# Turning the input chunks in SBUF before stage 1 of a Fourier mixing kernel

## The chip, the cores and the metric

The kernel runs on one core of a Trainium2 chip. A core has a matrix engine (TensorE, PE in the profile, with its weight loads listed as PEld), VectorE (DVE), ScalarE (ACT), GpSimd (POOL) and SyncE (SP), which run in parallel and wait for each other on semaphores. Each engine takes its instructions in order. Data lie in SBUF (128 partitions); matmuls write to PSUM. Transfers between HBM and SBUF are DMAs, issued here by SP (queue q1, "hardware") or by POOL (queue q0, "software", which can change the type of the data on the way), and run by 16 DMA engines that all queues share.

The metric is the time of one execution on the device in microseconds (us); lower is better.

## The reference

Input x is 8 batches of 3200 positions and 256 channels, float32. Two steps follow one another:

```python
X = np.fft.rfft(x, axis=1)
y = np.fft.irfft(X * (filt_r + 1j * filt_i)[None], n=3200, axis=1)     # circular filter, per channel
gate = 1 / (1 + np.exp(-causal_conv5(y, conv_w)))                      # 5 taps, per channel
out = (gate * (y @ w_val)) @ w_out
```

`causal_conv5` stands for the sum over k of `conv_w[k] * yp[:, k:k+S]`, where yp is y with four zero positions ahead. The output is float32, 8 x 3200 x 256.

## The kernel before, in words

**The transform.** 3200 is 128 x 25, and the position is written as n = 25 a + 128 r (mod 3200), a below 128 and r below 25. A transform of length 3200 is then one of length 128 over a and one of length 25 over r, with no factors between them. `load_x` (L80) brings a batch into a buffer `xb` with a as the partition: for each r one or two DMAs of rows, 49 in a batch, issued by POOL, which turn float32 into bf16. A row of `xb` is 25 x 260 elements (R x UW): 256 channels, and four columns of zeros. There are three such buffers.

**The channels** are split as d = 52 j + g, j below 5 and g below 52. One matmul takes one g, with all 25 r and 5 j: 125 columns. Eight chunks of a batch (`CH`) hold six or seven g each, 52 in all. The steps, by function:

- `s1` (L315): for each g of a chunk, the 125 columns are the stationary operand (the weights) and the table of cosines and sines `cf_t` (128 columns) is the moving one. In `xb` the columns of one g lie 52 elements apart. DVE evicts the result to `sob` (L324).
- `s2` (L327): the transform over r, four matmuls with tables of 125 x 125; ACT evicts (L338); DVE multiplies with the filter tables `fr_t` and `fm_t` and adds: `za`, `zb`, `z` (L349, L351, L352).
- `inva` (L356): back over r; ACT evicts to `u` (L370), one u per batch.
- `invb` (L375): back over the 128, per piece of three or four r (seven pieces to a batch); ACT evicts to `y` (L390). The first piece of a batch has POOL copy the four positions that the causal convolution needs ahead (L395, L397). It needs all of u.
- `conv` (L399, gate, ACT L411), `val` (L416, times the gate, DVE L428), `outp` (L434; even pieces are evicted by DVE, L445, odd ones by ACT, L448; SP stores them).

All PSUM tiles come from one pool of four buffers, so a tile's matmuls wait until the tile four places earlier has been evicted.

**The order.** The main loop (L470) counts chunks G over all batches, 64 in all. In a step each function handles another chunk or piece: `s1` chunk G, `s2` chunk G-1, `inva` chunk G-3, `invb`, `conv`, `val` and `outp` with lags of 11, 13, 14 and 15. In the loop they stand as invb, s1, conv, s2, val, inva, outp. A scheduler puts out the final order of each engine; on TensorE it is the order just given. Loads for later batches are put out ahead of each step, eight steps early.

**Before the loop** the tables are computed on DVE and ACT, and the filter is transformed to the layout of `fr_t` and `fm_t`. For each of its parts (real, imaginary) 13 x 65 rows are loaded straight (`gf`) and 12 x 65 more (`gh`) are reversed by matmuls (L233) and evicted into `gf` (L239 on ACT for the real part, L241 on DVE for the imaginary one). 52 matmuls turn `gf` (L249), again with 125 columns that lie 52 elements apart as weights; they are evicted to `ft` (L257, L259), and 25 matmuls (L270) expand that for the 25 residues, evicted by L284, L286 and L287.

Of the kernel before, what the change touches and what calls it, by code (L numbers as in the profile page):

```python
# [16 lines left out]
L = 128  # L17
# [14 lines left out]
def kernel(  # L32
# [36 lines left out]
    NX = 3  # L69
    xb = [cpool.tile([128, R, UW], BF16, name=f"xb{i}") for i in range(NX)]  # L70
    SW = 130
    sob = [cpool.tile([128, 7, SW], BF16, name=f"sob{i}") for i in range(4)]
    xsb = [cpool.tile([128, 2, 7, W], BF16, name=f"xsb{i}") for i in range(3)]
# [6 lines left out]
    def load_x(b, r):  # L80
        xt = xb[b % NX]
        na = min(L, -(-(S - L * r) // R))
        for a0, a1, s in ((0, na, L * r), (na, L, L * r + R * na - S)):
            if a1 > a0:
                src = bass.AP(tensor=x.tensor, offset=x.offset + (b * S + s) * D,
                              ap=[[R * D, a1 - a0], [1, D]])
                nc.gpsimd.dma_start(out=xt[a0:a1, r, 0:D], in_=src)  # L87
# [3 lines left out]
    with tc.tile_pool(name="gen", bufs=1) as g1, tc.tile_pool(name="gen2", bufs=2) as g2:  # L91
# [45 lines left out]
        gf, gh = [], []  # L137
        for i, f in enumerate((filt_r, filt_i)):
            g = g1.tile([65, R, UW], BF16, name=f"gf{i}")
            nc.vector.memset(g[:, :, D:UW], 0.0)  # L140
            nc.gpsimd.dma_start(
                out=g[:, 0:13, 0:D],
                in_=bass.AP(tensor=f.tensor, offset=f.offset,
                            ap=[[D, 65], [L * D, 13], [1, D]]))
            h = g1.tile([65, 12, D], BF16, name=f"gh{i}")
            nc.gpsimd.dma_start(
                out=h[...],
                in_=bass.AP(tensor=f.tensor, offset=f.offset + 64 * D,
                            ap=[[D, 65], [L * D, 12], [1, D]]))
            gh.append(h)  # L150
            gf.append(g)
        for t in xb:
            nc.vector.memset(t[:, :, D:UW], 0.0)
# [5 lines left out]
        for r in range(R):  # L159
            load_x(0, r)  # L160
# [67 lines left out]
        for i, g in enumerate(gf):  # L228
            gv = g[...].rearrange("p m d -> p (m d)")
            for h in range(3):  # L230
                ps = psum()
                for s in range(2):
                    nc.tensor.matmul(ps[0:65, 512 * s:512 * s + 512], lhsT=rev[0:65, :],  # L233
                                     rhs=gh[i][:, 4 * h + 2 * s:4 * h + 2 * s + 2, :],
                                     start=True, stop=True)
                dst = g[:, 13 + 4 * h:17 + 4 * h, 0:D]
                pv = ps[0:65, :].rearrange("p (m d) -> p m d", m=4)
                if i == 0:
                    nc.scalar.activation(dst, pv, AF.Copy)  # L239
                else:  # L240
                    nc.vector.tensor_copy(dst, pv)  # L241
            t1 = g1.tile([128, ND, 65], BF16, name=f"ft{i}")
            for h in range(4):
                ps = psum()
                for s, (o, n) in enumerate(((0, 6), (6, 7))):
                    for a in range(n):
                        d0 = 13 * h + o + a
                        lhs = gv[:, d0:d0 + (P2 - 1) * ND + 1:ND]
                        nc.tensor.matmul(ps[0:P2, 512 * s + 65 * a:512 * s + 65 * a + 65],  # L249
                                         lhsT=lhs, rhs=idb[0:65, 0:65],  # L250
                                         start=True, stop=True)
                for s, (o, n) in enumerate(((0, 6), (6, 7))):
                    dst = t1[0:P2, 13 * h + o:13 * h + o + n, :].rearrange(
                        "p g k -> p (g k)")
                    pv = ps[0:P2, 512 * s:512 * s + 65 * n]
                    if i == 0:
                        nc.scalar.activation(dst, pv, AF.Copy)  # L257
                    else:
                        nc.vector.tensor_scalar(dst, pv, sg[0:P2, 0:1], None, op0=ALU.mult)  # L259
            units = [(0, 3, 3), (3, 3, 3), (6, 3, 3), (9, 3, 3), (12, 3, 3),  # L260
                     (15, 4, 2), (19, 4, 2), (23, 2, 2)]
            for v in range(0, 8, 2):
                ps = psum()
                for s in range(2):
                    u0, nu, nt = units[v + s]
                    n = ND * nt
                    for uu in range(nu):
# [5 lines left out]
                            rhs=t1[0:P2, :, u:u + R * (nt - 1) + 1:R],  # L273
                            start=True, stop=True)
                    pv = ps[0:P2, 512 * s:512 * s + n * nu].rearrange(
                        "p (u g t) -> p g t u", u=nu, g=ND)
# [33 lines left out]
    ypool = ctx.enter_context(tc.tile_pool(name="yout", bufs=2))  # L310
# [4 lines left out]
    def s1(b, c):  # L315
        g0, nd = CH[c]
        xf = xb[b % NX][...].rearrange("p r d -> p (r d)")
        ps = psum()
        for i in range(nd):
            lhs = xf[:, g0 + i:g0 + i + (P2 - 1) * ND + 1:ND]  # L320
            nc.tensor.matmul(ps[0:P2, 128 * i:128 * i + 128], lhsT=lhs, rhs=cf_t[:, :],  # L321
# [53 lines left out]
    def invb(b, j):  # L375
        if j == 0:
            st[("Y", b)] = ypool.tile([128, 2, H + R, L], BF16, name="yt")
# [79 lines left out]
    for b in (0, 1):  # L457
        pass
    queue = [(b, r) for b in range(1, B) for r in range(R)]
    done = 0  # L460
# [9 lines left out]
    for G in range(NS + LAG_IB + 8):  # L470
        want = min(len(queue), (G + 8) * R // NF)
        while done < want:
            load_x(*queue[done])
            done += 1
# [5 lines left out]
        c = back(G, LAG_IB + 2)  # L480
        if c is not None:
            conv(*c)
# [5 lines left out]
        if 0 <= G - LAG_IA < NS:  # L488
            inva(*divmod(G - LAG_IA, NF))
        c = back(G, LAG_IB + 4)  # L490
        if c is not None:
            outp(*c)

# [29 lines left out]
```

## Time and profile before

| | |
|---|---|
| median of 3 runs | 458.85 us (458.5 to 459.55) |
| the profiled execution's own time | 458.49 us |
| its span in the trace | 456.8 us |
| first matmul of stage 1, batch 0 | 63.4 us |
| first `invb` of batch 0 | 97.05 us |
| last stage 1 matmul ends | about 406 us |
| one batch in the steady part (from the first `invb` of one to that of the next, 237.50 to 285.36 us) | 47.86 us |
| DMAs issued for x (L87) | 392, busy 201.8 us on POOL |

A profile shows one execution. In its page, a busy share is the time in which an engine had an instruction under way. A group's line names line, engine, operation, output <- input, shapes and count, then busy us and mean ns of one instruction, then the engine's idle time just before them and who ended it. In a timeline the first number is the start in us from the span's beginning, the second how long the merged instructions lasted. In a table of stretches each engine has its busy us, followed by TensorE's granted clock (1.00 is full), the DMA engines' share and GB/s. Matmuls are pipelined, so the recorded time of one is longer than the distance from its start to the next one's start; the distance is what counts on TensorE.

### The profile page before, as it was taken

To read this page: it belongs to the slowest core of one execution; us is meant where nothing else is said; L and a number is where in the kernel's file an instruction comes from. 1 tells how busy PE (TensorE), PEld (TensorE's weight loads), DVE (VectorE), ACT (ScalarE), POOL (GpSimd) and SP (SyncE) were. 2 spreads that over 40 slices of the span, in tenths; PEclk is the share of its full clock that TensorE was granted. 3 is DMA by queue.
4 is the path that set the end of the run, shared out by engine and by line. 5 is a ranking of instruction groups with operands and counts; after the bars stand their busy time and mean duration, and the time that the engine had idled before them with its cause. 6 is when DMAs were issued, how large, how long until landed. Compare 5 with 4: busy or idle time off the path is not lost.

```text
span 456.8 us, 10880 instructions
## 1 busy us (share of the span) xinstructions
PE 421.6 (92%) x4616; PEld 316.5 (69%) x4647; DVE 296.0 (65%) x465; ACT 255.4 (56%) x287; POOL 222.5 (49%) x440
## 2 busy tenths in 40 slices
PE   0797879988999999999999999999999999999994
PEld 0585868876776767777777777777777776766562
DVE  8116368875766766676767677657776766766364
ACT  1320144566666666666566656566666566657852
POOL 7499999899997439901991089500010001000100
PEclk9999999999999999999999999999999999999999
DMA  8966656465587438711782158421212022113324
GB/s 100 88 64 60 67 63 69 52 68 59 63 159 139 93 68 156 143 70 56 132 157 70 72 99 156 101 82 47 93 66 86 7 89 82 71 47 127 145 115 193
DMA packets 49713, 41.99 MB, mean 92 GB/s; under 512 B 13390, under 2 KB 42496, under 8 KB 49664
## 3 DMA queue, kind: packets, MB, share of 16 engines
q0 software_dynamic: 40288, 15.07, 30.9%
q1 hardware_dynamic: 9376, 26.22, 14.5%
q8 instruction: 36, 0.59, 0.5%
q14 instruction: 13, 0.11, 0.1%
HBM read 30.07 MB, written 26.21 MB: 123 GB/s over the span
## 4 chain that ended last, share of the span: by engine, by line
PE 72%; POOL 20%; DMA 3%; ACT 2%; issue 1%; DVE 1%; DVEq 0%; POOLq 0%
POOL xb L87 18%; PE ps L321 16%; PE ps L406 13%; PE ps L367 10%; PE ps L440 9%; PE ps L423 9%; PE ps L388 5%; PE ps L333 4%; DMA gh<-in_filt_i_dram 3%; PE ps L335 2%; PE ps L334 2%; PE ps L336 2%; ACT u L370 2%; POOL wv_t L296 1%; POOL wo_t L300 0%
## 5 line engine op out<-in xcount | busy, mean ns | idle before, releaser
L87 POOL DMA_DIRECT2D xb<-in_x_dram x392 | 201.8, 573 | 59.6 <-PE ps L321 43.3
L428 DVE TENSOR_TENSOR gv<-ps,gt 128x1024 bf16<-128x1024 f32 (+1 forms) x56 | 62.2, 1111 | 72.9 <-PE ps L423 69.5
L321 PE MATMUL ps<-cf_t,xb 128*125 128x128 f16 x416 | 101.6, 385 | 0.0
L321 PEld LDWEIGHTS <-xb 128*125 128x125 bf16 x416 | 96.6, 312 | 1.2 <-issue 0.2
L411 ACT ACTIVATE gt<-ps 128x1024 bf16<-128x1024 f32 (+1 forms) x56 | 52.2, 933 | 70.5 <-PE ps L406 63.4
L324 DVE CAST sob<-ps 125x768 bf16<-125x768 f32 x64 | 65.6, 1025 | 31.8 <-PE ps L321 31.4
L370 ACT ACTIVATE u<-ps 128x750 bf16<-128x750 f32 x64 | 67.0, 1047 | 31.8 <-PE ps L367 31.7
L338 ACT ACTIVATE xsb<-ps 125x780 bf16<-125x780 f32 x64 | 56.2, 878 | 27.2 <-PE ps L336 24.2
L406 PE MATMUL ps<-yt,dg_t 64*64 64x512 bf16 (+1 forms) x1120 | 65.3, 358 | 1.4 <-POOL yt L397 1.4
L397 POOL COPY yt<-yt 128x508 bf16<-128x508 bf16 x16 | 9.7, 643 | 113.1 <-ACT yt L390 113.1
L367 PEld LDWEIGHTS <-z 125*64 125x64 bf16 x1664 | 48.7, 110 | 23.1 <-issue 22.4
L367 PE MATMUL ps<-tb_t,z 125*64 125x125 f16 x1664 | 59.1, 220 | 0.0
L390 ACT ACTIVATE yt<-ps 128x1024 bf16<-128x1024 f32 (+1 forms) x56 | 52.1, 930 | 12.1 <-PE ps L388 11.3
L440 PE MATMUL ps<-wo_t,gv 128*128 128x256 bf16 x400 | 53.3, 274 | 0.9 <-DVE gv L428 0.9
L423 PE MATMUL ps<-yt,wv_t 128*128 128x512 bf16 (+1 forms) x193 | 50.8, 352 | 1.7
L349 DVE TENSOR_TENSOR za<-xsb,fr_t 125x792 bf16<-125x792 bf16 x64 | 38.7, 604 | 15.0 <-ACT xsb L338 15.0
L440 PEld LDWEIGHTS <-gv 128*128 128x128 bf16 x400 | 35.2, 98 | 10.7 <-DVE gv L428 1.2
L406 PEld LDWEIGHTS <-dg_t 64*64 64x64 bf16 x1120 | 28.0, 106 | 18.9 <-issue 2.3
L352 DVE TENSOR_TENSOR z<-za,zb 125x792 bf16<-125x792 bf16 x64 | 39.1, 611 | 0.8
L445 DVE COPY o<-ps 128x1024 f32<-128x1024 f32 (+1 forms) x32 | 36.8, 1151 | 3.9 <-PE ps L440 3.9
L351 DVE TENSOR_TENSOR zb<-xsb,fm_t 125x792 bf16<-125x792 bf16 x64 | 38.8, 607 | 0.0
L388 PE MATMUL ps<-ci_t,u 128*128 128x128 f16 x400 | 31.8, 219 | 4.1 <-ACT u L370 4.1
(93 smaller groups left out, 341.2 us busy)
## 6 DMA issues: line engine op xcount, KB each, us to landing
out_dram<-o SPq DMA_DIRECT2D x32, 512.0 KB, 2.9
out_dram<-o SPq DMA_DIRECT2D x24, 384.0 KB, 2.3
xb<-in_x_dram POOLq DMA_DIRECT2D x8, 64.0 KB, 2.4
xb<-in_x_dram POOLq DMA_DIRECT2D x8, 61.5 KB, 2.6
xb<-in_x_dram POOLq DMA_DIRECT2D x8, 61.0 KB, 2.5
xb<-in_x_dram POOLq DMA_DIRECT2D x8, 59.0 KB, 2.4
xb<-in_x_dram POOLq DMA_DIRECT2D x8, 58.5 KB, 2.9
xb<-in_x_dram POOLq DMA_DIRECT2D x8, 56.5 KB, 2.5
```

The source lines that it names most:

```text
L87: nc.gpsimd.dma_start(out=xt[a0:a1, r, 0:D], in_=src)
L321: nc.tensor.matmul(ps[0:P2, 128 * i:128 * i + 128], lhsT=lhs, rhs=cf_t[:, :], start=True, stop=True)
L324: nc.vector.tensor_copy(so[0:P2, 0:nd, 1:SW - 1], ps[0:P2, 0:nd * 128].rearrange("p (g k) -> p g k", g=nd))
L338: nc.scalar.activation(xs[0:P2, :, 0:nd, 0:65], ps[0:P2, :].rearrange("p (c n) -> p c n", c=2)[:, :, 0:65 * nd] .rearrange("p c (g k) -> p ...
L367: nc.tensor.matmul(ps[lo:lo + 64, o:o + P2], lhsT=z[0:P2, blk, i, s0:s0 + 64], rhs=tab, start=first, stop=not first)
L370: nc.scalar.activation(u[:, :, :].rearrange("p r (j g) -> p r j g", j=J)[:, :, :, g0:g0 + nd], ps[:, :].rearrange("p (g m) -> p g m", m=12 ...
L388: nc.tensor.matmul(ps[:, o:o + L], lhsT=u[:, r, 128 * dh:128 * dh + 128], rhs=cw_[:, sh:sh + L], start=True, stop=True)
L406: nc.tensor.matmul(ps[64 * dh:64 * dh + 64, 512 * r:512 * r + np_ * L], lhsT=dg_t[rows, dh, k, :], rhs=y[rows, dh, p0 + k:p0 + k + np_, :] ...
L411: nc.scalar.activation(g[:, :, 0:np_ * L], ps[:, :].rearrange("p (h n) -> p h n", h=2)[:, :, 0:np_ * L], AF.Sigmoid)
L423: nc.tensor.matmul(ps[:, 512 * eh:512 * eh + np_ * L], lhsT=wv_t[:, dh, 128 * eh:128 * eh + 128], rhs=y[:, dh, H + p0:H + p0 + np_, :], st ...
L428: nc.vector.tensor_tensor(gv[:, :, 0:np_ * L], ps[:, :].rearrange("p (h n) -> p h n", h=2)[:, :, 0:np_ * L], g[:, :, 0:np_ * L], op=ALU.mult)
L440: nc.tensor.matmul(ps[:, D * a:D * a + D], lhsT=gv[:, eh, L * a:L * a + L], rhs=wo_t[:, eh, :], start=(eh == 0), stop=(eh == 1))
```

## The change

Ahead of stage 1 each chunk is copied to a buffer `xpb`, four of which are in rotation, in the order of g, then (r, j); the 125 columns of one g are neighbours there. POOL makes these copies (`permute`) for batches 1 to 7, two steps ahead of `s1`. Batch 0 is loaded as float32 into a buffer `x0` of its own, 27 of its 49 DMAs by SP and 22 by POOL, and its eight chunks are turned by DVE (even ones) and ACT (odd ones).

Batch 1 is loaded by itself, batches 2 and 3, 4 and 5, 6 and 7 are loaded in pairs, two batches to a DMA; there are two buffers of two batches instead of three of one. `x0` gives its place to the tiles `yt` when the first batch is through.

The filter's columns are turned the same way: `gd` (the straight rows) is copied to `gp` by one instruction on ACT or DVE, and the reversed rows are evicted from PSUM into `gp` in 15 pieces instead of three per part, so that the weights of the 52 matmuls are neighbours. `ft` is laid out with g innermost.

In the loop, `conv` now stands behind `outp` and ahead of `inva`.

```diff
-    NX = 3
-    xb = [cpool.tile([128, R, UW], BF16, name=f"xb{i}") for i in range(NX)]
+    xb = [cpool.tile([128, 2, R, UW], BF16, name=f"xb{i}") for i in range(2)]
...
+    NP = 4
+    xpb = [cpool.tile([128, 7, P2], BF16, name=f"xpb{i}") for i in range(NP)]
...
-    def load_x(b, r):
...
+    def load_x(b, nb, r):
+        xt = xb[(b // 2) % 2]
+        for a0, a1, s in pieces(r):
+            src = bass.AP(tensor=x.tensor, offset=x.offset + (b * S + s) * D,
+                          ap=[[R * D, a1 - a0], [S * D, nb], [1, D]])
+            nc.gpsimd.dma_start(out=xt[a0:a1, b % 2:b % 2 + nb, r, 0:D], in_=src)
+
+    def load_first(xt, r):
+        for a0, a1, s in pieces(r):
+            n = a1 - a0
...
+            k = max(i for i in range(1, 17) if n % i == 0)
+            eng = nc.gpsimd if k < 5 else nc.sync
+            eng.dma_start(out=xt[a0:a1, r, 0:D], in_=src)
+
+    def permute(b, c, eng, src=None):
+        g0, nd = CH[c]
+        xt = xb[(b // 2) % 2][:, b % 2] if src is None else src[...]
+        dst = xpb[(NF * b + c) % NP][:, 0:nd, :].rearrange("p g m -> p m g")
+        sv = xt.rearrange("p r (j g) -> p (r j) g", j=J)[:, :, g0:g0 + nd]
+        if eng is nc.scalar:
+            nc.scalar.activation(dst, sv, AF.Copy)
+        else:
+            eng.tensor_copy(dst, sv)
...
-                dst = g[:, 13 + 4 * h:17 + 4 * h, 0:D]
...
+            q = gp[i]
+            ev(q[...].rearrange("p g m j -> p g (m j)")[:, :, 0:65].rearrange(
+                "p g n -> p n g"), gd[i][...].rearrange("p m (j g) -> p (m j) g", j=J))
...
+                for j in range(J):
+                    n = min(ND, D - ND * j)
+                    ev(q[:, 0:n, m0:m0 + 4, j].rearrange("p g m -> p m g"),
+                       pv[:, :, ND * j:ND * j + n])
...
-            t1 = g1.tile([128, ND, 65], BF16, name=f"ft{i}")
+            t1 = g1.tile([128, 65, ND], BF16, name=f"ft{i}")
...
-                        lhs = gv[:, d0:d0 + (P2 - 1) * ND + 1:ND]
...
+                                         lhsT=qv[:, 13 * h + o + a, :],
...
-        xf = xb[b % NX][...].rearrange("p r d -> p (r d)")
+        xp = xpb[(NF * b + c) % NP]
...
-            lhs = xf[:, g0 + i:g0 + i + (P2 - 1) * ND + 1:ND]
-            nc.tensor.matmul(ps[0:P2, 128 * i:128 * i + 128], lhsT=lhs, rhs=cf_t[:, :],
+            nc.tensor.matmul(ps[0:P2, 128 * i:128 * i + 128], lhsT=xp[:, i, :], rhs=cf_t[:, :],
...
+    loads = [(0, 1, 1, r) for r in range(R)]
+    loads += [(1 + 12 * r // R, 2, 2, r) for r in range(R)]
+    loads += [(16 + 14 * r // R, 4, 2, r) for r in range(R)]
+    loads += [(32 + 14 * r // R, 6, 2, r) for r in range(R)]
...
+        if G == 0:
+            permute(0, 0, nc.vector, x0)
+            permute(0, 1, nc.scalar, x0)
+        if G + 2 < NF:
+            permute(0, G + 2, nc.scalar if G % 2 else nc.vector, x0)
+        elif G + 2 < NS:
+            permute(*divmod(G + 2, NF), nc.gpsimd)
+        for g, b, nb, r in loads:
+            if g == G:
+                load_x(b, nb, r)
...
         if G < NS:
             s1(*divmod(G, NF))
-        c = back(G, LAG_IB + 2)
-        if c is not None:
-            conv(*c)
         if 0 <= G - 1 < NS:
             s2(*divmod(G - 1, NF))
...
         if c is not None:
             outp(*c)
+        c = back(G, LAG_IB + 2)
+        if c is not None:
+            conv(*c)
+        if 0 <= G - LAG_IA < NS:
+            inva(*divmod(G - LAG_IA, NF))
```

## The prediction

> **What bounds the kernel now.** I read the page's busy table first, then the table of stretches, the groups by shape, and the timeline of TensorE in one period. The busy table (busy us, share of the span, instructions) and one 25 us stretch of the steady part (PE, PEld, DVE, ACT, POOL) come first:
>
> ```profile
> PE 421.6 (92%) x4616; PEld 316.5 (69%) x4647; DVE 296.0 (65%) x465; ACT 255.4 (56%) x287; POOL 222.5 (49%) x440
> ...
> 300.00:325.00 25.00, 24.84 (x295) 18.41 (x295) 16.22 (x21) 16.05 (x18) 0.00 (x0) 1.00 0.16 64
> ```
>
> PE is busy 24.84 of 25 us, at full clock, while DVE and ACT work 16 of 25 and POOL may be idle. The steady part is bound by TensorE. Its groups by shape (busy us, mean ns, idle before):
>
> ```profile
> L321 PE MATMUL ps<-cf_t,xb 128*125 128x128 f16 x416 | 101.6, 385 | 0.0
> L321 PEld LDWEIGHTS <-xb 128*125 128x125 bf16 x416 | 96.6, 312 | 1.2 <-issue 0.2
> L388 PEld LDWEIGHTS <-u 128*128 128x128 bf16 x400 | 25.7, 97 | 8.2 <-ACT u L370 6.2
> L333 PEld LDWEIGHTS <-tb_t 125*125 125x125 f16 x64 | 9.0, 141 | 16.9 <-issue 16.9
> L284 DVE CAST fr_t<-ps 125x468 bf16<-125x468 f32 x5 | 4.3, 932 | 18.4 <-PE ps L270 18.4
> L286 ACT ACTIVATE fm_t<-ps 125x208 bf16<-125x208 f32 x1 | 0.6, 556 | 2.1 <-PE ps L270 2.1
> L284 DVE CAST fr_t<-ps 125x208 bf16<-125x208 f32 x1 | 0.5, 504 | 0.0
> ```
>
> A weight load of 125 columns that lie 104 bytes apart (52 bf16) is recorded at 312 ns; 125 neighbouring columns take 141, 128 neighbouring ones 97. The timeline of TensorE (start us, length) says what that costs:
>
> ```profile
> 237.50 0.63 PE L388 MATMUL ps<-ci_t,u 128*128 128x128 f16 x8 [0.43 <-ACT u L370]
> 237.96 1.70 PE L321 MATMUL ps<-cf_t,xb 128*125 128x128 f16 x7
> 239.59 1.27 PE L406 MATMUL ps<-yt,dg_t 64*64 64x512 bf16 x20
> ...
> 243.73 0.61 PE L388 MATMUL ps<-ci_t,u 128*128 128x128 f16 x8
> 244.18 1.48 PE L321 MATMUL ps<-cf_t,xb 128*125 128x128 f16 x6
> 245.50 0.36 PE L333 MATMUL ps<-sob,tb_t 125*125 125x455 bf16 x1
> ```
>
> From start to start, seven matmuls of L321 take 1.63 us and six 1.32, some 226 ns each. Eight of L388, with as many moving columns, take 0.45 us, 56 each. The record of a load is then about 86 ns longer than its claim on the engine (312 - 226), which leaves 141 - 86 = 55 ns for 125 neighbours, no more than the matmul.
>
> **The change, part by part.** The sum is made against the profiled execution, 458.49 us (span 456.8, 1.7 around it); the median shown is 0.36 higher.
>
> *Stage 1 weights.* I take 57 ns instead of 226, near L388's 56; the upper end is 141, if the load hid under nothing. A batch has 52 such matmuls: 8.8 us of its 47.86 (237.50 to 285.36). From the first invb at 97.05 on, 53 chunks remain, 344 matmuls: -58 us if nothing else binds (-29 at 141). TensorE: Matmul & The Clock Gate of the Trainium skill, section Weight-path perf modes, gives the fast load only to full 128-column weights, and its section LDWEIGHTS puts others at columns / 1.2 ns, an estimated 104 ns here; the 141 against 97 agrees that 125 columns are slower, but the 55 left above speaks against 104; by the rule the term would be -42.
>
> *What then is late.* A batch without the 8.8 us lasts 39.1. DVE works 16.2 to 17.8 of 25 us, 32.6 per batch, ACT 30.3: 83 and 77% instead of 68 and 63. Three waits follow.
> (a) Now conv stands ahead of inva, and invb of a batch's first piece follows inva directly; outp no longer lies between. That invb waits for the copy of u (1.09 us, behind gt's on ACT). 0.43 us becomes about 1.35: +0.9 for seven batches, +6.
> (b) Four PSUM buffers, seven uses a step. Where DVE evicts outp (even pieces) its order is gv, za, zb, o: 1.2 + 1.15 + 1.2 = 3.6 us from the end of val, and stage 1 of the next step wants that buffer after outp, conv, inva and invb, 3.4 us. I charge 0.3 us at four steps of a batch, 1.2, some +8 (0 to +20).
> (c) POOL. A permute has 750 or 875 elements. Bounds: 1.15 ns an element (L397: two copies of 508 in 1.16 us, runs of neighbours), 1.0 us; and 3.2 times that, 3.2 us, the factor of strided to neighbouring weight loads (312 to 97). I take 2.0 ns, from L284's 932 ns for 468 elements, the nearest scattered write: 1.75 us. It is four buffers ahead, so up to three steps of PE cover it. Loads stand before it in POOL's queue:
>
> ```profile
> 45.05 34.68 POOL L87 DMA_DIRECT2D xb<-in_x_dram  x67
> ```
>
> That is 0.52 us each, whatever the rows; 392 become 49 for batch 1 and 147 of twice the rows. The moving is the second price: 0.61 DMA share at 0.52 us gives 0.32 us for one, 0.63 for a double one. In the built order the last 49 loads stand around five permutes: 49 x 0.63 + 5 x 1.75 = 40 us against about eight steps of 4.9 us in which no new chunk is lacking: +2 (0 to +8). If the cover is gone, every missing us is PE's.
> Sum after 97 us: -58 + 6 + 8 + 2 = -42.
>
> *DVE against POOL.* Before, only one pair of POOL copies met DVE's multiplies:
>
> ```profile
> 106.35 1.30 DVE L352 TENSOR_TENSOR z<-za,zb 125x924 bf16<-125x924 bf16 x1
> ...
> 106.52 1.60 POOL L397 COPY yt<-yt 128x508 bf16<-128x508 bf16 x2
> ```
>
> z took 1.30 us instead of 0.64, the two copies 1.60 instead of 1.16 (zb just before also took 1.04, with no copy beside it that the trace shows). A waiting permute starts when stage 1 of four chunks earlier ends, and so does DVE's CAST of it (1.03 us), followed by gv (1.1): both read PSUM, and they cover 2.1 us. I charge nothing; without this cover the price is up to 1.75 us of DVE in each step, whose DVE time is 4.1 of 4.9. SBUF — State Buffer, section Who interferes with whom, in the Trainium skill says that a DVE instruction with two SBUF inputs and a GpSimd one that reads SBUF shut each other out for a whole instruction; the 1.30 agrees, and the rule speaks against this change.
>
> *First batch.* From 63.4 to 97.05 us eleven chunks run at 3.1 us, TensorE nearly full. TensorE sinks to about 2.1 a chunk, but DVE's CAST, za, zb, z take 2.6; with short waits 2.75, 30.3 us, plus two of DVE's four x0 permutes (750 x 2.0 = 1.5 us): 33.3 for 33.6. ACT's permutes (875 elements, the same rate) have room: ACT's 1.9 of 2.75. Nothing gained. POOL reaches the permute of batch 1 after 22 loads for x0, eight of weights (5 us), 49 + 21 loads: about 76 us; it is wanted at step 8, 63 + 22 = 85. That cover is 9 us; four loads and a permute a step (4.3 us) may then give 3 back.
>
> *Filter.* Its 104 strided loads (23.3 us of L249 on PE, one stretch of 11.65 per part) shrink: 13.0 us from first matmul to the last eviction become 6.2, bound by eight evictions of 0.5 to 0.65. But each three evictions of 1024 become fifteen of 208 or less: 15 x 0.556 for 2.84 on ACT, +5.5; 15 x 0.504 for 3.45 on DVE, +4.1. gd's own turn, 3380 elements, is 3.5 us at 1.04 ns and 6.8 at 2.0; it lies beside gh's landing (ACT) and TensorE's first part (DVE). Two x0 permutes on DVE stand ahead of the second part's evictions, +3. L270's stage is bound by evictions, -1. SP's 27 float32 loads share the DMA engines with the filter (26.22 MB took 14.5% of 16 engines, so 1.65 MB some 4 us, half ahead of gh): +2. The sum, -6.8 - 6.8 + 5.5 + 4.1 + 3 - 1 + 2, is 0. Bounds: -12 (writes at full rate) and +10 (gd late).
>
> *Drain.* 423 to 457 us has no stage 1; unchanged.
>
> In all 458.5 - 42 = 416.5; I say **416**.
>
> **The rivals.**
> 1. All of it arrives: no waits (b), (c), filter -5: 458.5 - 58 + 6 - 5 = 401, and 390 with the filter's lower bound. For it: DVE at 83% still leaves a sixth; against it: DVE 3.6 against 3.4.
> 2. Port contention makes DVE the bound: each step 4.1 + half a permute 0.9 + short waits 0.4 = 5.4, a batch 43.2 plus (a) 1 = 44: 3.7 x 6.6 = 24 off 458.5, 434. For it the 1.30; against it, the phase of CAST and gv.
> 3. The loads fall only part of the way: hidden under nothing, they cost between L388's record, 97 ns, and L333's, 141: -44 to -29, with waits (b), (c) mostly hidden under the longer stage and (a) kept: 421 to 435. For it: no row shows 125 neighbouring columns under 128 moving ones; against it the 55 ns. (The Trainium skill's section LDWEIGHTS, named above, would land here.)
> 4. Slower: POOL becomes the bound. It has 8 permutes and 24.5 loads x 0.63 = 15.4 us per batch. Against 47.86 that decides at 4.0 us per permute, or at 2.3 if each is also shut out for the 1.7 us of za, zb, z. At 3.2 us, shut out each time: 8 x 4.9 + 15.4 = 54.6, 6.7 x 6.6 = 44 more, 503. For it the 3.2 end and the 1.60 of the copies; against it that the change lets POOL run ahead, and that at 1.75 us even all shut out gives 43.
>
> **How the numbers follow.** Mine 0.48 (404 to 428); rival 1 0.17; rival 2 0.15; rival 3 0.10; slower 0.09; 0.01 for no change. 416 is the likeliest case. 394 to 446 leaves out about half of rival 1, a rest of rival 2, and rival 4. Faster by over 0.2% (0.9 us, about what the three runs can tell): 0.90; within 0.01; slower 0.09.
>
> **What would show it.** Right: stage 1 loads near 140 ns, 57 ns from start to start; a batch of 41 to 43 us; a wait of 1.0 to 1.5 us at a batch's first invb; permutes of 1 to 2 us; first stage 1 near 63, first invb near 97. Wrong: PE waiting for xpb, or for sob with DVE full; multiplies over 1 us; loads over 200 ns; stage 1 starting after 70.

## The result, and the profile after

The changed kernel takes **613.46 us** (median of four runs, 610.87 to 614.72) against 458.8 for the kernel before: a ratio of **1.336**, 95% interval 1.331 to 1.341. The forecast was 416 with a range of 394 to 446, faster with a chance of 0.90. It was wrong in sign and far outside its range. What stage 1 was to gain did come; the price on POOL was much higher than the forecast had it.

The profiled execution has a span of 609.1 us, 152.3 more than before. The busy table (busy us, share of the span, instructions), from the page of the changed kernel:

```profile
PE 379.7 (62%) x4616; PEld 260.9 (43%) x4647; DVE 435.1 (71%) x484; ACT 293.7 (48%) x304; POOL 440.0 (72%) x322
...
POOL 37%; PE 24%; DVE 14%; DMA 13%; issue 9%; ACT 2%; POOLq 0%; DVEq 0%; ACTq 0%
```

TensorE lost its 92% and is idle for more than a third of the time. The second line is the chain that ended last: POOL leads it. The same 25 us as before, in the table of stretches (PE, PEld, DVE, ACT, POOL, granted clock, DMA share, GB/s):

```profile
300.00:325.00 25.00, 20.99 (x301) 14.98 (x301) 23.71 (x25) 15.89 (x18) 21.48 (x18) 0.96 0.65 92
```

POOL went from 0 to 21.5 of 25 us and DVE from 16.2 to 23.7. The groups by shape say why:

```profile
L91 POOL DMA_DIRECT2D xb<-in_x_dram x196 | 202.7, 1117 | 19.2 <-DMA xb<-in_x_dram 19.0 <-POOL yt L430 0.3
L110 POOL COPY xpb<-xb 128x875 bf16<-128x875 bf16 x28 | 117.7, 4204 | 37.6 <-PE ps L356 37.6
L110 POOL COPY xpb<-xb 128x750 bf16<-128x750 bf16 x28 | 100.5, 3589 | 32.4 <-PE ps L356 30.8 <-issue 1.1 <-PE ps L371 0.5
L384 DVE TENSOR_TENSOR za<-xsb,fr_t 125x924 bf16<-125x924 bf16 x32 | 59.1, 1846 | 0.0
L356 PEld LDWEIGHTS <-xpb 128*125 128x125 bf16 x416 | 37.2, 165 | 71.1 <-POOL xpb L110 47.4 <-issue 22.3
L264 DVE COPY gp<-gd 65x3380 bf16<-65x3380 bf16 x1 | 14.7, 14718 | 0.0
L262 ACT ACTIVATE gp<-ps 65x208 bf16<-65x208 f32 x12 | 12.2, 1403 | 0.0
L264 DVE CAST gp<-ps 65x208 bf16<-65x208 f32 x12 | 11.5, 1222 | 0.0
```

A POOL copy takes 3.6 or 4.2 us (4.8 ns an element), a double load 1.12, the filter's small evictions 1.2 to 1.4 where 0.5 to 0.56 was forecast, the turn of gd (the filter's straight rows) 14.7. The weight loads of stage 1 fell from 312 to 165 ns. The timeline of TensorE (start, length) in a batch after the last load shows what that is worth:

```profile
434.43 0.63 PE L423 MATMUL ps<-ci_t,u 128*128 128x128 f16 x8 [1.16 <-ACT u L405]
434.89 0.57 PE L356 MATMUL ps<-cf_t,xpb 128*125 128x128 f16 x7
435.30 0.34 PE L368 MATMUL ps<-sob,tb_t 125*125 125x390 bf16 x1
```

Seven matmuls of stage 1 take 0.41 us from start to start, 58 ns each; before, 1.63.

DVE's multiplies are the last part. Here are DVE's timeline and then POOL's, for the same stretch:

```profile
384.68 1.23 DVE L463 TENSOR_TENSOR gv<-ps,gt 128x1024 bf16<-128x1024 f32 x1 [2.26 <-PE ps L458]
385.82 13.72 DVE L384 TENSOR_TENSOR za<-xsb,fr_t 125x924 bf16<-125x924 bf16 x1
399.46 0.63 DVE L386 TENSOR_TENSOR zb<-xsb,fm_t 125x924 bf16<-125x924 bf16 x1
```

```profile
376.76 14.64 POOL L110 COPY xpb<-xb 128x750 bf16<-128x750 bf16 x4
390.78 1.60 POOL L432 COPY yt<-yt 128x508 bf16<-128x508 bf16 x2
392.11 3.73 POOL L110 COPY xpb<-xb 128x750 bf16<-128x750 bf16 x1
395.20 0.66 POOL L430 MEMSET yt<- 128x8 bf16 x1
395.25 4.39 POOL L110 COPY xpb<-xb 128x875 bf16<-128x875 bf16 x1
```

One multiply that needs 0.63 us lasts 13.72, and ends at 399.54, when POOL's row of copies ends at 399.64. POOL's copies lie back to back, and the multiply ends only as their row does.

By stages, from the timelines (us; first `invb` of each batch):

| stage | before | after | longer by |
|---|---|---|---|
| to the first stage 1 (filter) | 63.4 | 77.8 | 14.4 |
| to the first `invb` (first batch) | 33.65 | 63.4 | 29.8 |
| the next four batches (loads until 377 us) | 188.3 | 293.25 | 104.9 |
| three batches, none with loads | 137.9 | 141.1 | 3.2 |
| from the last batch's first `invb` to the end | 33.5 | 33.6 | 0.1 |

### The profile page after: what moved, and what is told of

It is laid out like the page before. It is cut to its first block, busy times and chain, and to the rows that moved or that the text cites. A ratio compares the mean times of both kernels' runs of the same rounds, so it can differ in the third digit from the quotient of the medians.

```text
span 609.1 us, 10892 instructions
## 1 busy us (share of the span) xinstructions
PE 379.7 (62%) x4616; PEld 260.9 (43%) x4647; DVE 435.1 (71%) x484; ACT 293.7 (48%) x304; POOL 440.0 (72%) x322
## 3 DMA queue, kind: packets, MB, share of 16 engines
q0 software_dynamic: 134544, 15.61, 27.7%
## 4 chain that ended last, share of the span: by engine, by line
POOL 37%; PE 24%; DVE 14%; DMA 13%; issue 9%; ACT 2%; POOLq 0%; DVEq 0%; ACTq 0%
POOL xb L91 25%; DMA xb<-in_x_dram 10%; POOL xpb L110 9%; DVE za L384 6%; PE ps L441 5%; PE ps L458 4%; PE ps L402 4%; DMA gh<-in_filt_i_dram 3%; PE ps L475 3%; DVE o L480 3%; PE ps L423 2%; PE ps L356 2%; DVE z L387 2%; DVE zb L386 2%; POOL x L100 1%
## 5 line engine op out<-in xcount | busy, mean ns | idle before, releaser
L110 POOL COPY xpb<-xb 128x750 bf16<-128x750 bf16 (+1 forms) x56 | 213.8, 3897 | 70.0 <-PE ps L356 68.4
L91 POOL DMA_DIRECT2D xb<-in_x_dram x196 | 202.7, 1117 | 19.2 <-DMA xb<-in_x_dram 19.0
L384 DVE TENSOR_TENSOR za<-xsb,fr_t 125x792 bf16<-125x792 bf16 x64 | 102.4, 1600 | 5.1 <-ACT xsb L373 5.1
L441 PE MATMUL ps<-yt,dg_t 64*64 64x512 bf16 (+1 forms) x1120 | 72.3, 384 | 45.6 <-POOL yt L432 25.7
L356 PE MATMUL ps<-cf_t,xpb 128*125 128x128 f16 x416 | 42.6, 252 | 66.8 <-POOL xpb L110 46.2
L402 PE MATMUL ps<-tb_t,z 125*64 125x125 f16 x1664 | 66.8, 237 | 8.2 <-DVE sob L359 7.3
L402 PEld LDWEIGHTS <-z 125*64 125x64 bf16 x1664 | 55.8, 121 | 34.2 <-issue 31.1
L356 PEld LDWEIGHTS <-xpb 128*125 128x125 bf16 x416 | 37.2, 165 | 71.1 <-POOL xpb L110 47.4
L386 DVE TENSOR_TENSOR zb<-xsb,fm_t 125x792 bf16<-125x792 bf16 x64 | 59.2, 926 | 0.0
L387 DVE TENSOR_TENSOR z<-za,zb 125x792 bf16<-125x792 bf16 x64 | 58.4, 912 | 1.1
L368 PE MATMUL ps<-sob,tb_t 125*125 125x390 bf16 x64 | 26.8, 418 | 33.0 <-DVE sob L359 27.4
L475 PEld LDWEIGHTS <-gv 128*128 128x128 bf16 x400 | 39.7, 100 | 16.0 <-issue 2.3
## 6 DMA issues: line engine op xcount, KB each, us to landing
gd<-in_filt_i_dram POOLq DMA_DIRECT2D x1, 422.5 KB, 16.2
```

What stands on the lines that cost most here:

```text
L91: nc.gpsimd.dma_start(out=xt[a0:a1, b % 2:b % 2 + nb, r, 0:D], in_=src)
L110: eng.tensor_copy(dst, sv)
L356: nc.tensor.matmul(ps[0:P2, 128 * i:128 * i + 128], lhsT=xp[:, i, :], rhs=cf_t[:, :], start=True, stop=True)
L384: nc.vector.tensor_tensor(za[0:P2, :, 0:n], xv, frv.unsqueeze(1).to_broadcast((P2, 2, n)), op=ALU.mult)
L386: nc.vector.tensor_tensor(zb[0:P2, :, 0:n], xv[:, ::-1, :], fmv, op=ALU.mult)
L387: nc.vector.tensor_tensor(z[0:P2].rearrange("p c g k -> p c (g k)")[:, :, 0:n], za[0:P2, :, 0:n], zb[0:P2, :, 0:n], op=ALU.add)
```

## The experiments

The theory after the result: POOL is the bound while loads go on. Its busy time for each of seven batches is 213.8 / 7 = 30.5 us of copies and 202.7 / 7 = 29.0 of loads, and 1.9 for yt: 61.4, where TensorE needs some 40. The four batches with loads took more than that, 73.3 each. In them POOL is busy for 247.6 of 293.25 us; in the rest its copies wait for stage 1 to free their buffer (26.6 us), so that the two engines wait for each other, and its loads for earlier transfers (14.4 us). The rivals: the lock of DVE against POOL's copies; the dearer double loads; the order of POOL's queue, in which the copy of yt that conv waits for stands behind loads and copies; and the filter. On the chips used for them, the kernel before took 456.95 to 459.64 us. e1 to e10 and c1 were timed once each, c2 to c5 four times. The four runs of the changed kernel lie within 4 us, so differences of that size say nothing.

**e1: without POOL's copies**

```diff
-        elif G + 2 < NS:
-            permute(*divmod(G + 2, NF), nc.gpsimd)
```

> The changed kernel without the 56 POOL copies of batches 1 to 7: stage 1 then reads whatever batch 0 left in the four chunk buffers, so the output is not the reference's, while loads, filter and order of the loop stay. Theory A (the copies are the cost: each lasts 3.6 to 4.2 us on POOL, keeps DVE's two-input multiplies out while it reads SBUF, and stands in one queue with the loads): multiplies back at 0.57 to 0.64 us, a batch of 39 to 42 us, 410 to 435 us in all, the filter's 14 us still there. Rival B (the new place of conv ahead of inva and the four PSUM buffers cost as much): batches stay at 48 us or more, over 480 us. Rival C (the double loads are the cost): first batch stays near 60 us and batches with loads near 60, over 500 us.

Measured: 504.85 us, 109 less than the changed kernel. The first batch takes 34.3 us instead of 63.4, za is back at 602 ns, batches without loads take 40.5: theory A in these parts. But the time is far above its 410 to 435. It is where rival C had it, though not for rival C's reason, a slow first batch: one batch lasts 112 us. The waits of this kernel (us in total, times, longest):

```profile
PE ps L441 <- POOL yt L432: 77.3, 2, 69.3
POOL xb L91 <- DMA xb<-in_x_dram: 35.8, 12, 8.2
```

So the copies carry most of the loss, and the loads alone can still hold TensorE up through the order of POOL's queue.

**e2: one batch a load**

```diff
-                load_x(b, nb, r)
+                for i in range(nb):
+                    load_x(b + i, 1, r)
```

> The changed kernel with one batch per DMA in place of two (294 loads for batches 2 to 7 in place of 147). Theory C1 (a double load is the dearer form: the trace shows 134544 packets on the software queue in place of 40288, and 1.12 us of POOL for one in place of 0.57): packets back near 45000, 0.5 to 0.7 us a load, and 20 to 60 us less, 555 to 595 us. Rival C2 (the number of DMAs is what counts, twice as many stand ahead of the copies): 20 us or more slower than 613. Theory A alone (copies are nearly all of it): within 10 us of 613.

Measured: 561.38 us, 52 less, as theory C1 had it. The single loads keep POOL busy for 188.2 us, the double ones for 202.7, so only 14 us of the saving are POOL's busy time. What differs besides is the number of packets in POOL's DMA queue, 36864 for 134544 (before: 40288). These runs don't show why fewer packets should save more than that, only where the time goes: POOL's loads waited 19.0 us for earlier transfers in the changed kernel and 1.0 here, and TensorE's waits for xpb (46.2 us there) are gone, while those for DVE's o in stage 1 grow from 13.0 us to 38.2.

**e3: copies written in runs**

```diff
-        dst = xpb[(NF * b + c) % NP][:, 0:nd, :].rearrange("p g m -> p m g")
-        sv = xt.rearrange("p r (j g) -> p (r j) g", j=J)[:, :, g0:g0 + nd]
+        dst = xpb[(NF * b + c) % NP][:, 0:nd, :]
+        sv = xt.rearrange("p r (j g) -> p g (r j)", j=J)[:, g0:g0 + nd, :]
```

> The changed kernel whose copies (on POOL, DVE and ACT alike) go through the same elements in the order of the destination: writes are neighbours, reads lie 104 bytes apart, in place of reads in runs of 6 or 7 and writes 250 bytes apart. Theory W (the far writes make a copy slow on every engine: 4.7 ns an element on ACT, 4.8 on POOL, against 1.15 for a copy in runs): copies of 1.0 to 2.2 us on POOL, 1.0 to 1.5 on ACT, and with them most of the loss gone outside the filter and the double loads, 470 to 520 us. Rival R (POOL pays for any far step, read or write): still 3.3 us or more, 590 to 630 us.

Measured: 535.84 us, 78 less. The same elements go to the same places; the copy now reads 104 bytes apart and writes neighbours, where the changed kernel reads neighbours and writes 250 bytes apart (125 elements of two bytes; the expectations of two later runs call it 14 bytes, which is wrong). Groups by shape of this kernel:

```profile
L110 POOL COPY xpb<-xb 128x875 bf16<-128x875 bf16 x28 | 53.3, 1904 | 49.8 <-PE ps L356 49.8
L110 POOL COPY xpb<-xb 128x750 bf16<-128x750 bf16 x28 | 47.0, 1679 | 48.2 <-PE ps L356 41.8 <-PE ps L402 4.4 <-issue 2.0
```

2.2 ns an element instead of 4.8. ACT's copies of the first batch fell from 4.10 to 2.01 us in the same way. The batches without loads take 41.3 us, although the copies still run. So theory W holds for the copies on POOL, and rival R falls; the time is 16 us above W's range, and ACT's 2.01 above its 1.0 to 1.5.

**e4: before, with copies that nobody reads**

```diff
+        if NF <= G < NS:
+            permute(*divmod(G, NF))   # on POOL, xb[b % NX] to xpb
```

> The kernel before, with POOL making the same copies of batches 1 to 7 (read in runs, written 250 bytes apart, 3.6 to 4.2 us) into buffers that nobody reads; stage 1 stays as it was. Theory A, lock part: za, zb, z of 0.6 us grow to 0.9 to 1.9 on average, and TensorE waits for z and sob; together with the loads behind the copies (8 x 3.9 + 49 x 0.52 = 57 us of POOL per batch against 47.9) 520 to 570 us. Rival Q (only POOL's queue counts): the multiplies stay at 0.6 us and the batches last 57 us as long as loads are left, about 500 us. Rival N (the copies are harmless, since nobody waits for them): within 5 us of 459.

Measured: 608.72 us, 152 more than before and above every range that was named. PE waits for none of these copies and still uses the strided weights. DVE's timeline, then POOL's:

```profile
202.27 59.01 DVE L357 TENSOR_TENSOR za<-xsb,fr_t 125x924 bf16<-125x924 bf16 x1
261.20 0.63 DVE L359 TENSOR_TENSOR zb<-xsb,fm_t 125x924 bf16<-125x924 bf16 x1
```

```profile
204.08 14.64 POOL L321 COPY xpb<-xb 128x750 bf16<-128x750 bf16 x4
218.13 0.62 POOL L403 MEMSET yt<- 128x8 bf16 x1
218.17 43.20 POOL L321 COPY xpb<-xb 128x750 bf16<-128x750 bf16 x12
```

Sixteen copies and a memset in a row kept one multiply waiting for 57 us. I read this run as the price of the lock alone. That was too quick, as the next one shows.

**e5: before, with fills in their place**

```diff
-        nc.gpsimd.tensor_copy(dst, sv)
+        nc.gpsimd.memset(dst, 0.0)
```

> The kernel before with 56 POOL memsets in the places of the unused copies of the run before this one: same 750 or 875 two-byte writes 14 bytes apart, no reading of SBUF. Theory: what shuts DVE's two-input multiplies out is POOL's reading of SBUF, so za stays within 100 ns of its 604 ns mean and only the time that the memsets take from POOL's queue shows (at 3.9 us each POOL would need 8 x 3.9 + 28 = 59 us a batch, some 530 us in all; at 1 us each 457 to 465). Rival: the scattered writes load the memory itself, so za rises above 1000 ns as with the copies and the time comes near their 608.7.

Measured: 607.32 us, the same as with the copies, where the theory had some 530 for fills of about this length. The groups of this kernel:

```profile
L320 POOL MEMSET xpb<- 128x750 bf16 (+1 forms) x56 | 206.4, 4136 | 0.0
L356 DVE TENSOR_TENSOR za<-xsb,fr_t 125x792 bf16<-125x792 bf16 x64 | 38.4, 600 | 149.0 <-ACT xsb L345 149.0
```

The part on za held: beside writes of the same pattern that read nothing, za takes 600 ns, so POOL's reading is what shuts DVE's multiplies out. SBUF — State Buffer, section Who interferes with whom, of the Trainium skill says just that of a DVE instruction with two SBUF inputs: it contends with a GpSimd instruction that reads SBUF, not with one that only writes; the 600 ns beside fills against 2256 beside copies agrees. And yet the time is the same: PE waits 142.2 us in four stalls, up to 69.3, for yt's copy, which stands behind fills and loads on POOL. Take the lock away and the queue costs as much; the two prices do not add.

**e6: before, with the turned filter only**

```diff
-                dst = g[:, 13 + 4 * h:17 + 4 * h, 0:D]
...
+                for j in range(J):
+                    n = min(ND, D - ND * j)
+                    ev(q[:, 0:n, m0:m0 + 4, j].rearrange("p g m -> p m g"),
+                       pv[:, :, ND * j:ND * j + n])
```

> The kernel before with only the filter part turned as in the changed kernel (gd, gp, the evictions of 208 and 3380 elements); main loop, loads and first batch as before. Theory: the filter part alone puts the first stage 1 back by some 14 us (77.8 for 63.4 in the two profiles), and all of it is time: 457 + 14 = 471. Rival: the delay in the changed kernel came from x0's copies and transfers in front of the filter; then the first stage 1 starts before 68 us and the time stays under 462.

Measured: 472.16 us, 15.0 more than before; the first stage 1 starts at 76.6. The filter's loss is a term of its own, and it is all paid.

**e7: single loads and no copies**

```diff
-        elif G + 2 < NS:
-            permute(*divmod(G + 2, NF), nc.gpsimd)
...
-                load_x(b, nb, r)
+                for i in range(nb):
+                    load_x(b + i, 1, r)
```

> The changed kernel without the 56 POOL copies (stage 1 of batches 1 to 7 reads what the first batch's copies left in the buffers, so the output is not the reference's) and with one batch per load. Theory: with neither POOL copies nor double loads, nothing but the filter's 14 us, the turn of the first batch and the waits of the new order are left: batches of 40 to 41 us from the second on, no stall above 8 us, 420 to 440 us in all. Rival (loads of any form block yt's copy in POOL's queue): a stall of over 20 us at conv behind yt, and over 450 us.

Measured: 437.62 us. Batches without loads take 40.5 us, as with double loads. One stall of 11.1 us of conv behind yt is left, longer than the 8 that the theory allowed. Take off the filter's 15 as well and this stands near 423: the gain that the forecast saw in the weights is there.

**e8: fills in place of the copies, in the changed kernel**

```diff
-            permute(*divmod(G + 2, NF), nc.gpsimd)
+            b, c = divmod(G + 2, NF)
+            dst = xpb[(G + 2) % NP][:, 0:CH[c][1], :].rearrange("p g m -> p m g")
+            nc.gpsimd.memset(dst, 0.0)
```

> The changed kernel with its 56 POOL copies replaced by POOL memsets of the same places: same writes 14 bytes apart, about the same time on POOL (4.1 us each in the run with fills), but no reading of SBUF; stage 1 of batches 1 to 7 then gets zeros, so the output is not the reference's. Theory A (POOL's occupancy is the price, the lock on DVE only comes on top): while loads last a batch needs 8 x 4.1 + 24.5 x 1.1 = 60 us of POOL, so 560 to 610 us in all with za back at 600 ns; batches without loads 41 us. Theory B (the lock on DVE's multiplies is most of the price): with it gone the time falls to 505 or below, where the run without the copies stood.

Measured: 565.56 us, 48 less (45 between the spans of the two profiles). Groups of this kernel:

```profile
L514 POOL MEMSET xpb<- 128x750 bf16 (+1 forms) x56 | 209.1, 3810 | 32.8 <-PE ps L356 32.8
L384 DVE TENSOR_TENSOR za<-xsb,fr_t 125x792 bf16<-125x792 bf16 x64 | 39.5, 617 | 12.0 <-ACT xsb L373 12.0
```

za is back at its old time, so what is gone is the lock on DVE's multiplies (POOL's own time for the fills is 4.7 us less than for the copies). First batch: 44.4 us instead of 63.4. The last three: 118.6 instead of 141.1. The four between: 289.4 instead of 293.25, almost nothing. There POOL did get through its loads earlier, at 323 us instead of 377, but over the whole run TensorE waited 65.8 us for xpb (46.2 with the copies) and 42.0 for yt (25.7): what the lock no longer costs, POOL's queue takes. Theory A holds, with the lock on top worth 45 to 48 us; theory B's 505 is refuted. One row doesn't fit "no reading, no lock":

```profile
93.84 10.63 DVE L110 CAST xpb<-x 128x750 bf16<-128x750 f32 x1
```

This copy of x0, which takes 1.82 to 2.06 us elsewhere in this run, lasted 10.63 beside POOL's first two fills and the loads between them. What held it these runs don't show.

**e9 and e10: yt's copy off POOL, without and with POOL's copies**

```diff
-            nc.gpsimd.memset(y[:, :, 0:H, 0:1], 0.0)
+            nc.vector.memset(y[:, :, 0:H, 0:1], 0.0)
             for dh in range(2):
-                nc.gpsimd.tensor_copy(y[:, dh, 0:H, 1:L], y[:, dh, R:R + H, 0:L - 1])
+                nc.vector.tensor_copy(y[:, dh, 0:H, 1:L], y[:, dh, R:R + H, 0:L - 1])
```

> The run without POOL's copies (504.9 us, double loads kept; stage 1 of batches 1 to 7 reads old data, so the output is not the reference's) with yt's memset and its two copies on DVE instead of POOL. Theory (the 69 us stall at conv is only the order of POOL's queue: yt's copy stands behind double loads that wait for a free buffer): the stall goes and the time falls by 60 to 75 us, to 430 to 445, though the loads still take 200 us of POOL. Rival (the loads themselves are late, whatever stands behind them): nothing to 25 us is gained, with PE or ACT waiting for the first batches' data instead.

> The changed kernel with yt's memset and copies on DVE, all else kept. Theory (with the copies on it POOL is full, 60 us a batch while loads last, so leaving the queue helps little): 585 to 613 us, PE waiting for xpb instead. Rival (queue order is the price here too): below 560.

Measured: 423.56 us without the copies, 611.9 with them. Without, 81 us go (504.85 to 423.56), more than the 60 to 75 expected, although the loads take as long as in e1 (203.3 us there) and wait longer (35.8 there), which the groups of that kernel show:

```profile
L91 POOL DMA_DIRECT2D xb<-in_x_dram x196 | 203.2, 1076 | 48.2 <-DMA xb<-in_x_dram 47.3 <-issue 0.8
L432 DVE COPY yt<-yt 128x508 bf16<-128x508 bf16 x16 | 4.7, 334 | 0.0
```

So without POOL's copies, double loads cost TensorE nothing by themselves; what cost was that yt stood in a queue behind them. With the copies, the 2 us between 611.9 and 613.46 are within the spread of the runs. There conv's waits for yt (25.7 us) do go, but TensorE still waits 43.7 us for xpb, and its waits for DVE grow, on which yt's copies now run. So that pair shows no gain from leaving the queue, and doesn't separate a full POOL from a DVE that is shut out. yt's copies on DVE show the lock once more: 334 ns here, and 1791 in the run that has POOL's copies.

**c1 to c5: a version that beats both.** The kernel before, with x loaded by SP as float32 into two buffers (POOL's cast is no longer needed, since the copy to `xpb` casts), copies written in runs, and before's filter and loop order:

```diff
-                nc.gpsimd.dma_start(out=xt[a0:a1, r, 0:D], in_=src)
...
+                        nc.sync.dma_start(out=xt[c0:c1, r, 0:D], in_=src)
...
+    def permute(b, c):
+        g0, nd = CH[c]
+        dst = xpb[(NF * b + c) % NP][:, 0:nd, :]
+        sv = xb[b % NX][...].rearrange("p r (j g) -> p g (r j)", j=J)[:, g0:g0 + nd, :]
+        nc.gpsimd.tensor_copy(dst, sv)
```

> The kernel before with its filter and loop order, x loaded by SP as float32 into two buffers, and POOL's copies writing neighbouring elements for all eight batches; POOL issues no load of x. Theory (copies of 1.8 us that start early, a POOL queue free of loads, DVE lengthened to some 730 ns per za): batches of 40 to 42 us, first invb at 90 to 100, 400 to 418 us in all: faster than both kernels. Rival (DVE and POOL shutting each other out is the bound even with short copies): batches at 46 or more and 445 to 470. Rival (SP's queue: stores of o stand behind loads): waits of PE for o on DVE or ACT, one or more above 5 us.

Measured: 437.45 us. In this first form the first rows of the batch after next were loaded over rows which the last copy of a batch had still to read, so that its output is not the reference's; the work is otherwise the same. The time lies between the theory's 400 to 418 and the first rival's 445 to 470. The first batch took 47 us, the next six 42.6 on the mean, and DVE's z 1155 ns (611 in the kernel before); PE's only wait for o was of 0.4 us, so the rival of SP's queue falls.

```diff
-                if G < NF * (b - 1) - 4 + r // 4:
+                if G < NF * (b - 1) - 2 + r // 5:
...
-            nc.sync.dma_start(
+            nc.gpsimd.dma_start(
                 out=cw[:, dh, :],
```

> As c1, with the loads of a batch held back until the last copy of the batch two before is issued, and the taps of the convolution loaded from POOL's queue instead of behind x's loads on SP's. In c1 the first batch took 47 us from first stage 1 to first invb, of which 7 were a wait of PE for sob behind dg's 20 operations on DVE; the later batches took 43. Theory: the wait at the start goes, batches stay at 43 since DVE still meets the copies: 425 to 437, faster than before by 4 to 7%. Rival (the start was slow because of the copies alone): 436 to 440.

Measured: 431.12 us, ratio 0.939 (0.935 to 0.942). The first batch took 39.7 us, the next six 42.4 on the mean (41.0 to 46.3): theory.

```diff
+        e = "PAPDPAPD"[c]   # c3; "DADPADAP" in c4, "DADPDAAP" in c5
+        if e == "A":
+            nc.scalar.activation(dst, sv, AF.Copy)
+        else:
+            (nc.gpsimd if e == "P" else nc.vector).tensor_copy(dst, sv)
-        nc.gpsimd.tensor_copy(dst, sv)
```

> As c2, with two of a batch's eight copies on ACT, two on DVE, four on POOL. Work of a batch: DVE 32.6 + 2 x 1.0 + half the lock's 6.6 = 37.9, ACT 30.3 + 2 x 2.0 = 34.3, PE 39.1. Theory (the lock is what keeps c1 at 43): batches of 41 to 42, 415 to 428. Rival (a copy on DVE or ACT delays the evictions that PE waits for by as much as the lock did): batches of 43 or more, no better than c2.

Measured: 430.5 us, 0.937 (0.933 to 0.940): no better than c2 within the interval, so the rival, though the six batches after the first take 42.5 on the mean, between the theory's 42 and the rival's 43. DVE's copies of seven columns take 1.97 us, not 1.0.

> As c2, with three of eight copies on ACT, three on DVE, two on POOL. DVE 32.6 + 3.0 + a quarter of 6.6 = 37.3, ACT 30.3 + 6.0 = 36.3. Theory: as c3 or up to 5 us better, 412 to 426. Rival (copies in the queues of ACT and DVE delay evictions): worse than c3.

Measured: **425.47 us**, ratio **0.925** (0.920 to 0.930). Better than c3 and within the theory's range, and 34 us faster than the kernel before on the same chip.

> As c4, but DVE gets only pieces of six columns (0, 2, 4), ACT 1, 5, 6 and POOL 3, 7. DVE's copies cost 0.93 us for 750 elements and 1.96 for 875, so this takes 1.0 us a batch off DVE and puts 0.3 on ACT. Theory (DVE is what holds c4's batches at 41.8): 3 to 7 us less than c4, 417 to 423. Rival (other waits hold it): within 2 us of c4.

Measured: 425.9 us, 0.929 (0.924 to 0.934), the same as c4: the rival. DVE's time did fall, from 329.6 to 320.0 busy us, and the copies cost what they should, as the groups of c5 say:

```profile
L102 ACT ACTIVATE xpb<-xb 128x875 bf16<-128x875 f32 x16 | 32.3, 2021 | 1.1 <-PE ps L337 1.1
L104 DVE CAST xpb<-xb 128x750 bf16<-128x750 f32 x24 | 22.1, 928 | 0.0
```

But DVE's load isn't what holds these batches at 41.6 us, against the 40.5 of the runs without copies. Nor are longer waits: TensorE is busy for 39.63 of 41.66 us in a batch of c5 (268.78 to 310.44) and for 38.48 of 40.50 in one of e9 (269.62 to 310.12), so it stands idle for 2.0 us in both. The 1.2 us lie in the matmuls' own time, and c5 has the loop order of the kernel before, e9 that of the changed one. No run changes the order alone, so that it is the order isn't shown.

## Why the prediction was wrong

*Stage 1 weights: right.* 57 ns forecast, 58 measured (0.41 us for seven). Rival 3 is refuted by that row. The 104 ns estimated from TensorE: Matmul & The Clock Gate, section LDWEIGHTS, of the Trainium skill aren't what such a matmul costs here: that row has 58. The batch that the forecast built, 39.1 + 0.9 + 1.2 = 41.2 us, is 40.5 in e1, e7, e8 and e9.

*(a) and (b): right.* A wait of 1.16 us at a batch's first invb, forecast 1.35; and 40.5 - 39.1 - 0.7 leaves 0.7 us for (b), forecast 1.2. In e9 stage 1 waits for o 4.7 us in all, seven times, which agrees.

*(c) POOL: the step that failed.* A permute was priced at 1.75 us with bounds of 1.0 and 3.2; it takes 3.9 on the mean, outside both. The row it was taken from, L284's 932 ns for 468 elements, was called the nearest scattered write, but L284 writes runs of three neighbours (`units` has three u for those 468). The permute writes single elements, each 250 bytes from the last. That 1.75 is close to what a copy costs that writes neighbours (1.79 in e3) is chance: the row was of another engine, reading PSUM. The upper bound came from strided weight loads, which are reads. No copy of before wrote single elements far apart (a fill of DVE did, 104 of them 132 bytes apart in 0.145 us, and shows no such price), and the bound should have been left open upward rather than tied to a read. Double loads, forecast at 0.63 us, took 1.12. Together with yt POOL needs 61.4 us a batch where the forecast had 8 x 1.75 + 24.5 x 0.63 = 29.4, and the four batches with loads took 104.9 us more instead of some 27 less.

*DVE against POOL: charged nothing, wrong.* The cover was to be the phase: a permute starts with DVE's CAST of sob and is over with gv. At 3.9 us it isn't over, and copies in a row keep DVE out for all of them (13.72 us here, 59.01 in e4). The price named for the case without cover, one copy per step, assumed that DVE gets its turn after one copy. The rule of SBUF — State Buffer, section Who interferes with whom, in the Trainium skill that the prediction weighed was the right warning; in these runs a multiply waited for a whole row of copies, not for one. In the changed kernel the lock is worth 45 to 48 us (e8), nearly all of it in the first batch and the last three.

*Order of the queue: not seen.* The prediction counted the loads that stand ahead of a permute in POOL's queue, but not that yt's copy, which conv needs, stands in it too. Without POOL's copies that is worth 81 us (e1 against e9), with them nothing that can be told from the spread (e10).

*First batch: wrong by 30 us.* 33.3 forecast, 63.4 measured. Without POOL's copies it takes 34.3, so the step was right and what failed is again (c). POOL reached batch 1's first copy at 93.89 us, where the forecast had about 76, and then needed 7.3 to 10.4 us from one copy to the next, with four loads between them, where the forecast had 4.3.

*Filter: wrong by 14 us.* The sum of 0 took 0.556 and 0.504 us for an eviction of 208 elements, from L286 and L284 (runs again); the 208 here, single elements written far apart, take 1.40 and 1.22. That is 15 x 0.85 = 12.7 us more than forecast on ACT for its part, and 15 x 0.72 = 10.8 on DVE; the first stage 1 came only 14.4 us later, so part of it is hidden. gd's turn took 14.7 us, forecast 3.5 to 6.8: 4.4 ns an element, written far apart as well. e6 shows the term by itself, 15.0 us.

*Drain: right*, 33.6 for 33.5.

*Rival 4* (POOL becomes the bound, deciding at 4.0 us a permute, or 2.3 if shut out each time) had the mechanism. Its formula with the measured sizes gives 8 x 3.9 + 24.5 x 1.12 + 8 x 1.7 = 72 us a batch, and the four batches with loads took 73.3 on the mean; that the lock's 13.6 belong in it is not borne out, for e8's four took 72.4 each without the lock. Nine in 100 was too low: of its two deciding prices 2.3 lay inside the bounds, and 4.0 just beyond one that rested on no like row.

*A sum.* Rival 1's second figure, 390, doesn't follow from its terms: with the filter at -12 they give 458.5 - 58 + 6 - 12 = 394.

## What to carry to other kernels

In these runs a copy that reorders elements was cheap or dear by its writing side: iterate in the order of the destination, so that it writes neighbours and reads far apart, and check that a row taken for its price writes in the same way. On an engine that also issues loads, add up its whole queue per period before costing an edit by waits, and look for small instructions in that queue that another engine waits for. Beside two-input work on DVE, look at how POOL's copies lie, not only at their average share: a row of them held one multiply for all of its length. Whether a gap behind each copy would help no run here tried; c4 moved six of the eight to other engines.

## What the runs showed of the hardware

- Single 2-byte elements written 250 bytes apart cost 4.8 ns each on POOL, 4.7 on ACT (875 in 4.10 us), and 4.4 in gd's turn on ACT as on DVE (3380 in 14.7 us). DVE's copies of x0 paid less, 2.4 to 2.7 (750 in 1.82 to 2.06 us in e7). A fill with the same writes and no reading takes 3.8 us on the mean on POOL in e8 and 4.1 in e5, as long as the copy. Written in runs, read far apart: 2.2 on POOL (104 bytes, e3), 2.3 on ACT (208 bytes, from float32). SBUF — State Buffer, section Specifications (TRN2), in the Trainium skill, has lines of 16 bytes and a penalty for each access that crosses to a new one. The copies agree; with reads far apart they show much less of it than with writes far apart.
- A row of POOL's copies keeps a two-input instruction of DVE out to the row's end: one 0.63 us multiply of DVE lasted 13.72 us beside POOL's row of copies in the changed kernel, and 59.01 beside sixteen copies in e4. A DVE copy with one input is held up too: 1791 ns with POOL's copies about (e10), 334 without (e9).
- DVE's copy in runs from float32 takes 0.93 us for 750 elements (c5) and 1.97 for 875 (c3), a jump that 875/750 does not explain.
- TensorE's granted clock is a mean of 0.86 over the span of the changed kernel and 0.996 in e9. In the changed kernel it is 0.74 to 0.79 from the first stage 1 to the third batch's first `invb` (77.78 to 295.92 us), where TensorE is busy for 121.7 of 218.1 us, and 1.00 in the last full batch, busy for 35.65 of 39.18. But it is 1.00 ahead of that too, where TensorE is busy for 24.2 of 77.8 us, so idleness alone doesn't set it.
